# A long convolution and a state-space layer on one core: four more C blocks by DMA-transpose, and a new task order

## The chip, the cores and the metric

The kernel runs on one core of a Trainium2 chip. A core has TensorE (PE, matrix products into PSUM), VectorE (DVE), ScalarE (ACT), GpSimd (POOL) and SyncE (SP). Here POOL and SP do almost nothing but start DMA transfers, which sixteen DMA engines of the core carry out. The metric is device time in microseconds (us) of one execution, compared by medians.

## The reference

Two independent layers share one kernel. Each has 2048 positions and 1024 channels; the results stand side by side in an output of 2048 x 2048 in bf16.

```
# layer A: short convolution, gate, long convolution by FFT, gate
k_shift = sum over t<4 of k_pad[:, t:t+S, :] * shift_k[:, 3-t]
kv = k_shift * v
y = irfft(rfft(kv, 2S) * rfft(ssm_k, 2S))[:S] + kv * ssm_D
a = q * y
# layer B: complex diagonal state space
Lam_bar = exp(dt * Lam);  B_bar = ((Lam_bar - 1) / Lam)[:, None] * (B_re + i B_im)
Bu = einsum("bld,pd->blp", x, B_bar)
h_t = Lam_bar * h_(t-1) + Bu_t
b = 2 * einsum("blp,dp->bld", h, C_re + i C_im).real + x * Dskip
out = concatenate([a, b], axis=-1)
```

## The kernel before

Everything is cut into named tasks. A list of some 1,700 names, ORDER (lines 67 to 171), is written out by hand or by a planner beforehand; the kernel walks through it (`for task in ORDER.split()`) and issues each task's instructions. So every engine, and every engine's queue of transfers, gets its work in the order of this list, each waits only for its own next instruction, and the list decides which work stands in front of which. Nothing is planned at run time. Tasks carry indices after the name.

**Layer B** is done in sixteen chunks i of 128 positions. `bl.j.w` loads a block of B (j of eight, w real or imaginary), `bT` turns it by eight TensorE transposes into a PSUM tile of pool ps_t (two buffers), `bc` copies it to BT. The first ten such blocks are staged in the tile CT, which later holds C. `xl` and `xt` load and turn the first three chunks of x; `x.i` copies them to xT, or, from the fourth chunk, brings the chunk by DMA-transpose. `U.i.jp` (line 478) is 32 matmuls of 128 columns into ps_u (two buffers), `ue` (480) its copy on ScalarE. VectorE then does the recurrence of the chunk: `r1` (490, product with the table Z1), `r2` (499, sum), `ca` (504, carry), `sc` (510, two scans), `cm`, `cy` (carry for the next chunk), `r3` and `r4` (490, 523). `y.i.dh.part` (534, 539) is the product with C into ps_y (one buffer), each of the two halves dh in four parts; `ye` (549) copies it out and `yst` stores it, `ysh` for the last chunk. The tables come from `tab`, `sin`, `par_rest`, `z1`, `eo`, `stt`, `z2`, which use slots 5 to 7 of CT as working space until the last `stt` and `eo`.

**C** reaches CT in sixteen blocks (d of eight, w of two). A block goes one of two ways. Either `cl` (449) loads 256 KB into a staging buffer of tag ld (five buffers, shared with the last six B blocks and with `v`), `cT` (430) turns it with eight TensorE transposes and `cc` (453, ScalarE) copies it to CT; or `cx` (451) brings it by one DMA-transpose, issued from SP's queue, straight into CT:

```
E["cx"] = lambda d, w: nc.sync.dma_start_transpose(CT[:, :, w, d * P:(d + 1) * P], Cv[w][d * P:(d + 1) * P, :])
E["cT"] = lambda d, w: tr_(("cn", d, w), ("cp", d, w))
E["cc"] = lambda d, w: nc.scalar.copy(CT[:, :, w, d * P:(d + 1) * P], st.pop(("cp", d, w))[:])
```

A cx writes to all eight rows of CT, so it waits for the staged B blocks and for the tables. y.i.0 needs the blocks with d below 4, y.i.1 those from 4.

**Layer A** is an FFT in three stages over sixteen residues n2. `k` and `v` load; `kvm` (579), `kva` (586), `kvb` (592), `kvc` (597) on VectorE give kv in a tile acc (two buffers), `am.n2.w` (603) multiplies it with the table F1t into ps_a (three buffers), `ae` (612) copies, `ast` (POOL) stores to the DRAM tile Ys_kv. `hl`, `hT`, `hc`, `hm` (649), `he` (657), `hst` (664) do the same for the filter, with `hd` adding the skip term; tile ysbh has three buffers, Ys_h is the DRAM tile. Stage two, over 32 groups g: `lh`, `l`, `lw` load, `sh` and `sk` (684) multiply, `she` and `ske` copy to hab or hb and x16, `sw` (711, 712, POOL) swaps halves by DMA, `pr` (717, VectorE) multiplies, `sa` (726) goes back into ps_t, `sae` (737) copies into vsb (two buffers, two groups each), and `vst` (739, POOL) stores to the DRAM tile Vs. Every load `vl` of stage three needs all sixteen vst. Stage three: `vl`, `a3` (756), `a3e` (764), then `qm` (775) or, for the last three residues, `qp` (770) multiplies with q (`ql`), and `ost` or `oth` stores.

The remaining tasks `ld_*`, `wb`, `wbe`, `par_T`, `p32`, `exp`, `dve2`, `dve3`, `sm_pre`, `sin0`, `dd` are small and prepare parameters and weights.

Of the kernel before, what the change touches and what calls it, by code (L numbers as in the profile page):

```python
# [66 lines left out]
bl.0.1 bl.1.1 ld_w xl.0 k.-3 ld_par xl.1 ld_F bl.7.1 ld_G bl.0.0 k.-2 bT.0.1 bl.4.1 xl.2 bT.1.1 bc.0.1 k.-1 bl.2.1  # L67
wb.4 bc.1.1 bl.5.0 par_T wb.5 bl.4.0 p32 wb.6 bl.1.0 exp1 xt.0 bl.3.1 bl.2.0 xt.1 bl.3.0 wbe.4 dve2 k.0 x.0 bl.6.0
dve3 wb.7 x.1 x.3 wbe.5 bT.0.0 sm_pre exp2 wbe.6 hl.0.0 xt.2 wbe.7 bl.7.0 bc.0.0 tab.0 bl.5.1 wb.0 hl.0.1 wb.1 k.1 x.2
dd bT.7.1 wbe.0 bT.5.0 wbe.1 bl.6.1 tab.1 wb.2 wb.3 bc.5.0 v.0 bc.7.1 x.4 tab.2 bT.1.0 wbe.2 bT.2.1 wbe.3 bc.1.0 tab.3  # L70
k.2 x.5 bc.2.1 sin0 U.0.0 tab.4 hl.1.0 k.3 kvm.0 k.4 sin.2 bT.2.0 U.1.0 bc.2.0 ue.0.0 par_rest k.5 sin.4 bT.3.1 U.2.0
ue.1.0 kva.0 eo.0 bT.3.0 U.3.0 bc.3.1 bc.3.0 kvb.0 ue.2.0 stt.0 z1.1 bT.4.0 bT.4.1 kvm.1 ue.3.0 U.1.1 eo.1 U.3.1
ue.1.1 bc.4.1 k.6 bc.4.0 kva.1 z1.0 U.0.1 kvc.0 ue.3.1 kvb.1 eo.2 kvm.2 bT.6.0 bT.5.1 v.1 bc.6.0 am.0.0 U.2.1 ae.0.0
bc.5.1 ue.0.1 z1.2 kvm.3 bT.6.1 am.0.1 am.0.2 am.0.3 U.1.2 ae.0.2 ae.0.1 ue.2.1 stt.2 ast.0.0 ae.0.3 bT.7.0 ue.1.2
ast.0.1 bc.6.1 U.0.2 v.2 bc.7.0 stt.1 cl.0.1 cl.2.0 cl.1.0 U.0.3 kva.2 eo.3 kvc.1 ue.0.2 kvb.2 am.1.0 cl.2.1 ue.0.3
U.2.2 stt.3 kvc.2 z2 cT.2.0 r1.0 cl.3.1 cT.0.1 k.7 ae.1.0 U.3.2 cl.3.0 cc.2.0 cl.0.0 cx.5.0 ue.2.2 kva.3 cT.2.1 cc.0.1
U.2.3 cx.6.0 r2.0 ue.3.2 cc.2.1 hd.0 am.2.0 sc.0 k.8 hT.0.0 ue.2.3 cx.4.1 U.3.3 ae.2.0 hc.0.0 cx.7.1 am.2.1 am.1.1
ue.3.3 hT.0.1 ae.2.1 am.1.2 cx.7.0 cT.0.0 ae.1.1 ast.2.0 am.1.3 hc.0.1 U.1.3 ast.1.0 kvb.3 ae.1.2 cm.0 r3.0 ae.1.3
U.4.0 cc.0.0 ast.1.1 ue.1.3 kvm.4 cT.3.1 ue.4.0 cT.1.0 cc.3.1 hm.0.0.0 hm.0.0.1 v.3 hm.0.0.2 U.4.1 he.0.0.0 r4.0 k.9
he.0.0.1 cl.1.1 he.0.0.2 cx.6.1 hst.0.0.0 cy.0 kva.4 U.4.2 ue.4.1 cc.1.0 v.5 r1.1 cT.3.0 am.2.2 hm.0.0.3 cc.3.0 v.6  # L80
U.4.3 cx.4.0 kvc.3 ue.4.2 r2.1 he.0.0.3 ae.2.2 hT.0.2 v.4 hst.0.0.1 ue.4.3 U.5.0 ca.1 cx.5.1 sc.1 v.9 hm.0.1.0 am.2.3
ue.5.0 hm.0.1.1 U.5.1 hc.0.2 he.0.1.0 he.0.1.1 U.5.2 ae.2.3 hst.0.1.0 kvb.4 ue.5.1 cm.1 r3.1 ast.2.1 cT.1.1 ue.5.2
hT.0.3 cc.1.1 am.3.0 hm.0.1.2 hl.1.1 hm.0.1.3 x.6 U.5.3 kvm.5 ae.3.0 he.0.1.2 he.0.1.3 hl.2.0 hc.0.3 v.7 hst.0.1.1
hm.0.2.0 am.3.1 hm.0.2.1 r4.1 k.10 ue.5.3 y.0.0.0 he.0.2.0 he.0.2.1 y.0.0.1 kva.5 ae.3.1 hst.0.2.0 y.0.0.2 kvc.4 hd.1
am.3.2 kvm.6 y.0.0.3 ast.3.0 ae.3.2 am.3.3 am.4.0 ye.0.0 hm.0.2.2 hT.1.0 ae.3.3 y.0.1.0 ae.4.0 kvb.5 ast.3.1 he.0.2.2
kva.6 am.4.1 y.0.1.1 ae.4.1 r1.2 ast.4.0 hm.0.2.3 y.0.1.2 he.0.2.3 hc.1.0 hm.0.3.0 hst.0.2.1 y.0.1.3 he.0.3.0 kvc.5
hT.1.1 ye.0.1 cy.1 am.4.2 r2.2 v.8 hm.0.3.1 am.4.3 ae.4.2 yst.0 y.1.0.0 ae.4.3 kvb.6 he.0.3.1 am.5.0 ast.4.1 ca.2
y.1.0.1 kvc.6 ae.5.0 hst.0.3.0 kvm.7 v.11 hm.0.3.2 hm.0.3.3 k.11 am.5.1 he.0.3.2 U.6.0 x.7 he.0.3.3 ae.5.1 hst.0.3.1
hc.1.1 sc.2 v.13 am.5.2 y.1.0.2 k.12 ue.6.0 ast.5.0 ae.5.2 y.1.0.3 hm.1.0.0 am.5.3 ye.1.0 U.6.1 ae.5.3 he.1.0.0
ast.5.1 kva.7 hT.1.2 ue.6.1 hm.1.0.1 hm.1.0.2 am.6.0 r3.2 he.1.0.1 y.1.1.0 he.1.0.2 hst.1.0.0 ae.6.0 hm.1.0.3 U.6.2  # L90
# [749 lines left out]
```

## Time and profile before

| | |
|---|---|
| median of nine runs | 384.27 us (382.0 to 386.89) |
| the profiled execution, in all | 383.0 us |
| its span, first to last instruction | 380.9 us |
| TensorE busy | 362.2 us (95%) |
| VectorE busy | 329.9 us (87%) |
| ScalarE busy | 277.0 us (73%) |
| GpSimd busy | 124.9 us (33%) |
| moved by DMA | 101.15 MB, mean 266 GB/s |
| transposes on TensorE, line 430 | 112 from ld, 80 from CT, 24 from ysb |
| DMA-transposes | 13 for xT, 8 for CT |

The profile is of one execution. Its span is 2.1 us shorter than that execution's time. Busy shares are averages over stages that differ; matmuls are pipelined, and the end of one is modelled, so that the spacing between their starts says more than their lengths. A row of the windows gives, for a stretch of time, the busy microseconds of each engine, the granted TensorE clock, the share of time in which the sixteen DMA engines had packets, and what they moved. A wait row names who waited, for whom, how long in all, how often, and the longest.

### The profile page before, as it was taken

What the parts mean: (1) busy time and instruction counts of PE and PEld (TensorE: products, weight loads), DVE (VectorE), ACT (ScalarE), POOL (GpSimd) and SP (SyncE); (2) the same over time, 40 slices, a digit from 0 to 9 for tenths busy, and PEclk for the clock granted to TensorE, in tenths of its full rate; (3) what the DMA queues carried; (4) which work ended last, traced back from release to release, by engine and by line L of the source; (5) the groups of instructions that cost most, each with busy time, mean ns of one, the idle gap of its engine ahead of it and who ended that gap; (6) DMA issues with size and microseconds to landing.
All of it is one profiled execution on the core that took longest, in us unless ns stands there. A gap on an engine that the chain in (4) does not pass through costs nothing.

```text
span 380.9 us, 9007 instructions
## 1 busy us (share of the span) xinstructions
PE 362.2 (95%) x3553; PEld 247.5 (65%) x3553; DVE 329.9 (87%) x341; ACT 277.0 (73%) x511; POOL 124.9 (33%) x215
## 2 busy tenths in 40 slices
PE   4999999999999999999999999999999999799992
PEld 2699999966777767777666455545645755564440
DVE  3899989999999997999999999989983597099843
ACT  2889888778788777777427888998899988437232
POOL 3000102346365645547204322352342523102111
PEclk9999999999999999999999999999999999999998
DMA  8998699997686866455978989999999956889988
GB/s 245 336 322 246 179 214 258 258 338 245 213 269 244 214 168 199 148 189 172 315 178 264 266 300 278 359 285 296 313 282 360 303 200 189 295 299 361 405 326 293
DMA packets 60772, 101.15 MB, mean 266 GB/s; under 512 B 28445, under 2 KB 31517, under 8 KB 60730
## 3 DMA queue, kind: packets, MB, share of 16 engines
q1 hardware_dynamic: 47274, 59.51, 54.7%
q0 software_dynamic: 13376, 41.05, 31.0%
q8 instruction: 28, 0.46, 0.5%
q14 instruction: 14, 0.11, 0.1%
q10 hardware_dynamic: 80, 0.01, 0.0%
HBM read 53.10 MB, written 33.55 MB: 228 GB/s over the span
## 4 chain that ended last, share of the span: by engine, by line
PE 73%; DMA 9%; ACT 5%; DVE 5%; issue 4%; POOL 1%; SPq 0%; DVEq 0%; ACTq 0%; POOLq 0%
PE ps_u L478 24%; PE ps_y L534 23%; PE ps_a L684 5%; PE ps_t L726 5%; PE ps_t L430 3%; DMA Vs<-vsb 3%; PE ps_a L603 3%; DMA ysb<-in_B_x_dram 3%; PE ps_a L649 3%; PE ps_t L627 2%; PE ps_u L534 2%; DMA Ys_h<-ysbh 2%; PE ps_y L539 1%; PE ps_a L756 1%; DVE h L510 1%
## 5 line engine op out<-in xcount | busy, mean ns | idle before, releaser
L534 PE MATMUL ps_y<-CT,h 128*128 128x512 bf16 x480 | 125.1, 379 | 0.7 <-ACT yo L549 0.5
L478 PE MATMUL ps_u<-xT,BT 128*128 128x128 bf16 x2048 | 124.9, 220 | 0.0
L478 PEld LDWEIGHTS <-BT 128*128 128x128 bf16 x2048 | 120.1, 99 | 6.5 <-issue 0.2
L534 PEld LDWEIGHTS <-h 128*128 128x128 bf16 x512 | 46.3, 98 | 46.1 <-DVE h L523 0.7
L510 DVE TENSOR_TENSOR_SCAN h<-rtab,h 128x1024 bf16<-128x1024 f32 x32 | 71.5, 2277 | 0.3
L664 POOL DMA_DIRECT2D Ys_h<-ysbh x64 | 46.2, 724 | 39.2 <-ACT ysbh L657 39.0
L480 ACT CAST u<-ps_u 128x512 bf16<-128x512 f32 x64 | 38.5, 602 | 26.6 <-PE ps_u L478 26.6
L737 ACT CAST vsb<-ps_t 128x512 bf16<-128x512 f32 x64 | 39.1, 643 | 9.6 <-DMA Vs<-vsb 5.0
L490 DVE TENSOR_TENSOR mt<-u,Z 128x4096 bf16<-128x4096 bf16 x16 | 36.6, 2286 | 9.6 <-ACT u L480 9.6
L657 ACT CAST ysbh<-ps_a 128x512 bf16<-128x512 f32 x64 | 35.9, 611 | 10.3 <-DMA Ys_h<-ysbh 5.4
L614 POOL DMA_DIRECT2D Ys_kv<-ysb x32 | 17.9, 561 | 77.5 <-ACT ysb L612 75.4
L612 ACT CAST ysb<-ps_a 128x512 bf16<-128x512 f32 x64 | 37.1, 605 | 6.2 <-PE ps_a L603 5.8
L706 ACT CAST x<-ps_a 128x512 bf16<-128x512 f32 x64 | 37.7, 632 | 2.5 <-PE ps_a L684 2.4
L490 DVE TENSOR_TENSOR mt<-h,Z 128x4096 bf16<-128x4096 bf16 x16 | 36.6, 2285 | 0.1
L717 DVE TENSOR_TENSOR hab<-x,hab 128x2048 bf16<-128x2048 bf16 x18 | 21.7, 1215 | 10.4 <-DMA hab<-hab 6.7
L579 DVE TENSOR_TENSOR mt<-kring,wbc 128x4096 bf16<-128x4096 bf16 (+3 forms) x16 | 30.1, 1884 | 0.0
L549 ACT CAST yo<-ps_y 128x512 bf16<-128x512 f32 x30 | 18.2, 608 | 14.7 <-PE ps_y L534 12.8
L539 PE MATMUL ps_y<-Dd,xT 128*128 128x128 bf16 x120 | 26.3, 219 | 0.0
L726 PEld LDWEIGHTS <-wts 128*128 128x128 bf16 x128 | 12.3, 98 | 17.3 <-issue 4.4
L603 PE MATMUL ps_a<-acc,F1t 128*128 128x512 bf16 x64 | 22.1, 379 | 0.1
L694 ACT CAST hab<-ps_a 128x512 bf16<-128x512 f32 x36 | 21.3, 622 | 0.9 <-PE ps_a L684 0.7
L649 PE MATMUL ps_a<-hT,F1t 128*128 128x256 bf16 x128 | 21.3, 272 | 0.6 <-ACT ysbh L657 0.4
(125 smaller groups left out, 518.2 us busy)
## 6 DMA issues: line engine op xcount, KB each, us to landing
Ys_kv<-ysb POOLq DMA_DIRECT2D x32, 256.0 KB, 3.1
Ys_h<-ysbh POOLq DMA_DIRECT2D x64, 128.0 KB, 3.1
hk<-Ys_h SPq DMA_DIRECT2D x16, 512.0 KB, 6.2
l2k<-Ys_kv SPq DMA_DIRECT2D x16, 512.0 KB, 5.6
Vs<-vsb POOLq DMA_DIRECT2D x16, 512.0 KB, 6.0
vv<-Vs SPq DMA_DIRECT2D x32, 256.0 KB, 5.8
hab<-hab POOLq DMA_DIRECT2D x36, 128.0 KB, 5.6
kring<-in_A_k_dram SPq DMA_DIRECT2D x16, 256.0 KB, 5.3
```

What stands on the lines that cost most here:

```text
L478: nc.tensor.matmul(pu[:, w, jl, :], BT[:, 2 * jp + jl, w, d, :], xT[:, d, :], start=(d == 0), stop=(d == ND - 1))
L480: E["ue"] = lambda i, jp: nc.scalar.copy(st["u", i][:, :, 2 * jp:2 * jp + 2, :], st.pop(("pu", i, jp))[:])
L490: nc.vector.tensor_mul(m, s_, win(Z))
L510: nc.vector.tensor_tensor_scan(gf[:, a, :], rt1, gf[:, a, :], 0.0, ALU.mult, ALU.add)
L534: nc.tensor.matmul(py[:], h[:, 1 - w, j, :], CT[:, j, w, dh * 512:(dh + 1) * 512], start=(j == 0 and w == 0), stop=(j == NJ - 1 and w == 1))
L603: nc.tensor.matmul(st["pa", n2, w][:], F1t[:, cc, :], st["kv", n2][:, dh * 512:(dh + 1) * 512], start=True, stop=True)
L612: nc.scalar.copy(st["ysb", n2, cc][:, dh * 512:(dh + 1) * 512], st.pop(("pa", n2, w))[:])
L649: nc.tensor.matmul(pt[:, cc * DQ:(cc + 1) * DQ], F1t[:, cc, :], st["hT", qd, n4][:, w, :], start=True, stop=True)
L657: nc.scalar.copy(st["yh", qd, n4, w // 2][:, :, w % 2, :], st.pop(("pa", qd, n4, w))[:].rearrange("p (c d) -> p c d", c=2))
L664: gpd(Ys_h[cc, n0:n0 + 2, :, qd * DQ:(qd + 1) * DQ].rearrange("n k d -> k n d"), t_[:, cc, :, :])
L706: nc.scalar.copy(st["x16", g][:, w * 512:(w + 1) * 512], st.pop(("ps", "l2k", g, w))[:])
L737: nc.scalar.copy(st["vsb", gq][:, gi, w * 512:(w + 1) * 512], st.pop(("ps", "v", g, w))[:])
```

## The change

Only ORDER differs; all functions, buffers and sizes are the same. The tasks cl, cT and cc of the blocks with d = 2 and d = 3 are gone, and cx.2.0, cx.2.1, cx.3.0 and cx.3.1 are there instead: twelve blocks come by DMA-transpose and four (d = 0 and 1) by TensorE. In addition the whole list is in a new order, on every engine. Both lists are too long to show; these are the stretches around the first U, the C blocks, the residues 10 to 15 of layer A, the end of stage two, and the end.

```
-bl.0.1 bl.1.1 ld_w xl.0 k.-3 ld_par xl.1 ld_F bl.7.1 ld_G bl.0.0 k.-2 bT.0.1 bl.4.1 xl.2 bT.1.1 bc.0.1 k.-1 bl.2.1
-wb.4 bc.1.1 bl.5.0 par_T wb.5 bl.4.0 p32 wb.6 bl.1.0 exp1 xt.0 bl.3.1 bl.2.0 xt.1 bl.3.0 wbe.4 dve2 k.0 x.0 bl.6.0
-dve3 wb.7 x.1 x.3 wbe.5 bT.0.0 sm_pre exp2 wbe.6 hl.0.0 xt.2 wbe.7 bl.7.0 bc.0.0 tab.0 bl.5.1 wb.0 hl.0.1 wb.1 k.1 x.2
-dd bT.7.1 wbe.0 bT.5.0 wbe.1 bl.6.1 tab.1 wb.2 wb.3 bc.5.0 v.0 bc.7.1 x.4 tab.2 bT.1.0 wbe.2 bT.2.1 wbe.3 bc.1.0 tab.3
-k.2 x.5 bc.2.1 sin0 U.0.0 tab.4 hl.1.0 k.3 kvm.0 k.4 sin.2 bT.2.0 U.1.0 bc.2.0 ue.0.0 par_rest k.5 sin.4 bT.3.1 U.2.0
...
-U.2.2 stt.3 kvc.2 z2 cT.2.0 r1.0 cl.3.1 cT.0.1 k.7 ae.1.0 U.3.2 cl.3.0 cc.2.0 cl.0.0 cx.5.0 ue.2.2 kva.3 cT.2.1 cc.0.1
-U.2.3 cx.6.0 r2.0 ue.3.2 cc.2.1 hd.0 am.2.0 sc.0 k.8 hT.0.0 ue.2.3 cx.4.1 U.3.3 ae.2.0 hc.0.0 cx.7.1 am.2.1 am.1.1
...
-hT.3.2 hc.3.1 am.10.3 hm.3.0.0 hm.3.0.1 y.4.0.1 ae.10.3 kvb.12 he.3.0.0 r2.5 ast.10.1 am.11.0 he.3.0.1 hT.3.3 ae.11.0
...
-she.31.0 sa.27.0 cm.13 r3.13 ske.30.0 sa.27.1 she.31.1 U.14.2 ye.12.0 sw.31 sae.27.0 sae.27.1 cy.13 r4.13 sk.30.1
-sk.29.1 ue.14.2 vst.13 sa.28.0 ske.29.1 sk.31.0 sa.28.1 sae.28.0 pr.29 y.12.1.0 ske.30.1 sae.28.1 sk.31.1 pr.30
-ske.31.0 sa.29.0 ql.0 ske.31.1 sa.29.1 ql.5 ql.1 y.12.1.1 sae.29.0 ql.6 sae.29.1 ql.2 pr.31 ql.4 sa.30.0 vst.14
-sa.30.1 sae.30.0 y.12.1.2 sae.30.1 sa.31.0 sa.31.1 sae.31.0 U.15.1 sae.31.1 vst.15 y.12.1.3 ue.15.1 U.14.3 ye.12.1
...
-y.15.1.0 a3e.2.0 a3e.11.0 y.15.1.1 a3e.2.1 ye.15.0 qm.2 y.15.1.2 ql.14 ost.2 qp.15.0 ql.10 y.15.1.3 ql.11 qp.15.1
-ql.13 a3.14.0 qm.3 ye.15.1 a3.10.0 a3.14.1 ost.3 a3.11.1 a3.12.0 a3e.11.1 vl.13 a3e.10.0 ql.8 ql.12 oth.15.0 oth.15.1
-qm.11 ost.11 a3e.12.0 qp.14.0 qp.14.1 a3.8.0 oth.14.0 a3.10.1 oth.14.1 ysh.0 a3.12.1 ysh.1 a3e.10.1 a3e.12.1 a3.8.1
-qm.10 a3e.8.0 qm.12 ost.10 a3e.8.1 a3.13.0 ost.12 a3.13.1 qm.8 ost.8 qp.13.0 qp.13.1 oth.13.0 oth.13.1
...
+xl.0 xl.1 ld_w bl.0.1 bl.1.1 ld_par bl.3.0 ld_F bl.2.0 bl.1.0 ld_G k.-3 xt.0 bl.0.0 xl.2 xt.1 k.-2 x.0 k.-1 wb.0 x.1
+bl.5.0 wb.1 wbe.0 bl.3.1 par_T wb.2 wbe.1 x.3 p32 bT.1.1 exp1 bT.2.0 bc.1.1 k.0 wbe.2 bl.5.1 wb.4 dve2 bl.4.1 bc.2.0
+bT.1.0 dve3 bl.4.0 tab.0 k.1 wbe.4 bl.2.1 wb.5 bc.1.0 bl.6.0 xt.2 sm_pre bl.7.1 wbe.5 x.4 wb.6 exp2 bT.0.0 x.2 tab.1
+dd wb.7 hl.0.0 wbe.6 bT.0.1 bc.0.0 hl.0.1 k.2 k.3 wb.3 wbe.7 bc.0.1 bT.3.0 hl.1.0 sin0 bl.6.1 tab.2 U.0.0 x.5 tab.3
...
+bc.4.1 ue.0.1 stt.2 bT.6.1 ue.2.1 cT.0.0 U.1.2 kvm.2 z2 cc.0.0 cx.7.1 U.0.2 kvc.0 ue.1.2 kva.1 v.2 am.0.0 v.1 am.0.1
+ue.0.2 U.2.2 k.7 bc.6.1 ae.0.0 cx.4.0 ae.0.1 kvb.1 ast.0.0 kva.2 bT.7.0 cx.2.1 ue.2.2 U.3.2 bc.7.0 kvm.3 v.3 cx.2.0
+am.0.2 am.0.3 ue.3.2 U.0.3 ae.0.2 kvb.2 ae.0.3 cl.1.1 kva.3 ast.0.1 cx.5.1 U.3.3 ue.0.3 kvc.2 r1.0 cT.1.0 ue.3.3
+hT.0.0 cl.0.1 cc.1.0 U.1.3 cx.7.0 kvc.1 hc.0.0 r2.0 cx.3.1 am.1.0 am.1.1 ue.1.3 U.4.0 sc.0 ae.1.0 ae.1.1 v.5 ast.1.0
+k.8 am.1.2 cx.4.1 am.1.3 ue.4.0 U.4.1 ae.1.2 ae.1.3 cx.6.0 ast.1.1 am.2.0 hm.0.0.0 ue.4.1 cT.0.1 kvb.3 ae.2.0 cx.3.0
...
+hst.0.0.0 r4.0 am.2.2 k.9 hm.0.0.2 ue.2.3 cx.6.1 hT.0.2 ae.2.2 hm.0.0.3 hT.0.3 kvc.3 he.0.0.2 U.4.3 r1.1 he.0.0.3
+cx.5.0 hc.0.2 hst.0.0.1 hm.0.1.0 hl.1.1 hm.0.1.1 ue.4.3 v.4 hm.0.1.2 kva.4 U.5.0 v.8 v.6 cy.0 r2.1 U.5.1 ue.5.0 ca.1
...
+ye.4.0 am.10.0 hT.3.3 kva.12 he.2.3.2 y.4.1.0 he.2.3.3 ae.10.0 kva.13 hst.2.3.1 am.10.1 am.10.2 am.10.3 ae.10.1
+y.4.1.1 kvb.12 ae.10.2 ast.10.0 ae.10.3 kvc.11 hm.3.0.0 hm.3.0.1 x.10 y.4.1.2 he.3.0.0 ast.10.1 r1.5 he.3.0.1 am.11.0
+hm.3.0.2 hst.3.0.0 hm.3.0.3 x.12 ae.11.0 y.4.1.3 hc.3.2 kvc.12 am.11.1 U.9.0 he.3.0.2 r2.5 he.3.0.3 ae.11.1 hst.3.0.1
+ca.5 ye.4.1 am.12.0 sc.5 hm.3.1.0 ue.9.0 U.9.1 ae.12.0 ast.11.0 he.3.1.0 yst.4 am.11.2 hm.3.1.1 ue.9.1 am.11.3 U.9.2
+he.3.1.1 ae.11.2 hst.3.1.0 ae.11.3 kvb.13 am.12.1 hm.3.1.2 ue.9.2 cm.5 ast.11.1 hm.3.1.3 r3.5 U.9.3 he.3.1.2 he.3.1.3
+ae.12.1 hst.3.1.1 hc.3.3 am.12.2 hm.3.2.0 kvm.14 hm.3.2.1 ue.9.3 ast.12.0 ae.12.2 he.3.2.0 am.12.3 he.3.2.1 hm.3.2.2
+kvc.13 ae.12.3 hm.3.2.3 hst.3.2.0 r4.5 v.15 am.13.0 he.3.2.2 ast.12.1 kva.14 he.3.2.3 y.5.0.0 ae.13.0 hst.3.2.1
+am.13.1 kvm.15 y.5.0.1 ae.13.1 ast.13.0 am.13.2 am.13.3 hm.3.3.0 ae.13.2 y.5.0.2 ae.13.3 kvb.14 he.3.3.0 hm.3.3.1
+ast.13.1 kva.15 hm.3.3.2 y.5.0.3 he.3.3.1 hst.3.3.0 he.3.3.2 hm.3.3.3 kvc.14 he.3.3.3 r1.6 am.14.0 ye.5.0 am.14.1
+am.14.2 hst.3.3.1 ae.14.0 y.5.1.0 ae.14.1 am.14.3 ast.14.0 y.5.1.1 cy.5 kvb.15 ae.14.2 r2.6 ae.14.3 y.5.1.2 ast.14.1
+y.5.1.3 kvc.15 ca.6 am.15.0 sc.6 lh.0 am.15.1 am.15.2 ae.15.0 lh.2 U.10.0 ae.15.1 lh.1 ast.15.0 am.15.3 U.10.1 ue.10.0
...
+ske.29.0 r1.13 sk.29.1 sk.30.0 sae.28.0 sa.27.1 ske.29.1 sk.30.1 sa.28.1 sae.27.1 U.15.1 ske.30.0 vst.13 pr.29
+ske.30.1 sae.28.1 pr.30 sk.31.0 y.12.0.3 ske.31.0 ue.14.1 sk.31.1 r2.13 sa.29.0 ye.12.0 ql.6 sa.29.1 ql.0 ske.31.1
+ql.5 y.12.1.0 ca.13 sae.29.0 ql.1 pr.31 ql.2 sae.29.1 ql.4 sa.30.0 ue.15.1 vst.14 sa.30.1 sc.13 sae.30.0 y.12.1.1
+sae.30.1 sa.31.0 sa.31.1 sae.31.0 y.12.1.2 sae.31.1 U.15.2 vst.15 cm.13 r3.13 y.12.1.3 ue.15.2 U.15.3 ye.12.1 yst.12
...
+y.15.0.2 y.15.0.3 y.15.1.0 y.15.1.1 a3e.12.0 y.15.1.2 a3e.11.0 qm.8 y.15.1.3 a3e.11.1 a3e.10.0 ost.8 qm.11 a3e.10.1
+a3.13.0 ql.15 ost.11 ye.15.0 a3.15.0 qp.13.0 ye.15.1 a3.12.1 a3.13.1 qm.10 oth.13.0 a3e.12.1 ysh.0 a3.14.0 qp.13.1
+ost.10 a3.15.1 qm.12 a3.14.1 ost.12 qp.14.0 qp.14.1 oth.14.0 oth.13.1 qp.15.0 ysh.1 oth.14.1 qp.15.1 oth.15.0 oth.15.1
```

## The prediction

> **What bounds the kernel now.** I read the busy line and the slices first, then the chain of waits, then the windows, the wait list and the instructions in order of time. On the page, TensorE leads and the chain runs through it:
>
> ```profile
> PE 362.2 (95%) x3553; PEld 247.5 (65%) x3553; DVE 329.9 (87%) x341; ACT 277.0 (73%) x511; POOL 124.9 (33%) x215
> ...
> PE   4999999999999999999999999999999999799992
> ...
> PE 73%; DMA 9%; ACT 5%; DVE 5%; issue 4%; POOL 1%; SPq 0%; DVEq 0%; ACTq 0%; POOLq 0%
> ```
>
> Busy time of a pipelined PE is not proof, so I counted its work by spacing. The chain in order of time (start, length, engine, tile, line, count) gives unhindered runs:
>
> ```profile
> 38.96 0.65 PE ps_a L603 x3
> 39.60 1.79 PE ps_u L478 x32
> ...
> 47.41 0.89 PE ps_t L430 x16
> ...
> 81.59 0.86 PE ps_y L534 x4
> ```
>
> That is 56 ns for a 128-column matmul, 216 ns for a 512-column one. Over all groups of the page (2048 + 128 + 216 + 128 narrow ones, 512 + 64 + 128 + 128 + 64 wide ones, 128 of 256 columns, 8 of wb) the sum is 351 us. The span is 380.9. The other 30 us are: 3.3 before the first matmul; 11 until about 22 us (waits, and matmuls at half pace: eight transposes take 1.0 us there, 0.45 later, with the clock row at 1.00 throughout); 2.3 between 22 and 200 us; 6.7 after that; 7.0 after the last matmul. So TensorE has almost no hole to fill: a new order can lose much and win little. VectorE is full too, and transfers are full just where the C blocks come:
>
> ```profile
> 30.00:40.00 10.00, 10.00 (x172) 9.53 (x169) 9.90 (x11) 9.25 (x20) 0.00 (x0) 1.00 0.69 239
> 50.00:60.00 10.00, 10.00 (x166) 9.50 (x164) 8.47 (x9) 8.58 (x14) 1.62 (x3) 1.00 1.11 227
> 60.00:70.00 10.00, 10.00 (x171) 9.79 (x169) 9.93 (x9) 7.44 (x12) 2.92 (x4) 1.00 1.24 251
> 230.00:260.00 30.00, 30.00 (x219) 16.77 (x217) 28.21 (x23) 26.65 (x54) 11.71 (x22) 1.00 0.99 319
> ```
>
> (Window, length, then busy us of PE, PEld, DVE, ACT, POOL, clock, DMA share, GB/s.) Two stalls in the middle and at the end matter below:
>
> ```profile
> 152.19 0.69 DVE L592 TENSOR_TENSOR acc<-mt 128x1024 bf16<-128x1024 bf16 x1 [2.49 <-PE ps_a L603]
> ```
>
> ```profile
> ACT ysbh L657 <- DMA Ys_h<-ysbh: 5.4, 5, 2.2
> ...
> ACT vsb L737 <- DMA Vs<-vsb: 5.0, 3, 3.6
> ...
> PE ps_t L726 <- ACT vsb L737: 3.2, 2, 2.6
> ```
>
> **The change, part by part**, against the profiled execution (span 380.9, 383.0 in all, 1.3 under the median 384.27).
>
> 1. *TensorE transposes removed.* Four cT tasks, 32 transposes: 4 x 0.45 = **-1.8 us** of the 351. PE is packed there, so I take all of it; bounds -1.8 and 0 (if PE then waits for something else).
>
> 2. *Copies removed.* Four cc on ScalarE at 1.03 us (L453): -4.1 us on an engine busy 7.4 to 9.3 of 10 us. No PE wait of before names them: 0; bounds -1 and 0.
>
> 3. *Transfers.* Four loads of 256 KB (cl) go, four DMA-transposes (cx) come. On SP's queue a cl takes 0.4 us, a cx 1.24 to 3.5 (eight took 14.9 in all), so about +6 us of a queue that paused for about 2 us three times between 31 and 44 us and for over 3 at 71 to 75. Between 50 and 70 us the DMA share is 1.11 and 1.24 at 227 and 251 GB/s; at 319 GB/s the share was 0.99. By bytes those windows would have needed 0.70 and 0.78: 8.7 us too much over eight transposes, 1.1 us each, +4.4 us for four more. The cover is the slack at 30 to 50 (share 0.69, 0.67) and the late use: the first y task reads C at 78.4 us. In the new order the last cx that y.0.0.0 needs (cx.3.0) follows cT.1.0's buffer (about 51 us) behind four others: 51 + 5 x 2.4 (48.76 to 53.5 held two) + 6.1 to land = 69, and PE reaches y.0.0.0 at about 75. Behind them wait k.9, hl.1.1, v.4; kvc.4 wants v.4 near 81. Cost 0; bounds 0 and +5 (the 8.7 repeated, less that slack).
>
> The row says 0.45 us of TensorE and 1.03 of ScalarE per block against 4.2 to 6.1 us of landing by DMA. [...]
>
> The order moves nearly every task on POOL's queue too, but its issues are the same in both (Ys_h, Ys_kv, Vs, hab, outputs); I price them only where a buffer turns on them (5 and 6).
>
> 4. *Start.* U.0.0 began at 19.31. New order: xt first, six bT instead of seven before U.0.0. Walking the two ps_t buffers by the rows (1.0 us for eight cold transposes, 1.01 ACT and 0.69 DVE per evacuation): wb.0 at 7.0 as before (its weights land then), bT.1.1 at 8.8, bT.1.0 at 11.2, xt.2 at 12.4 to 13.7 (its load has 2.9 MB ahead instead of 2.6), then bT.0.0, bT.0.1, bT.3.0: U.0.0 at 17.0 to 18.2. PE's own work ahead of it is 0.45 less, already counted, so **-0.9**; bounds -1.9 and +1.5 (a load one landing row, 1.5 us, later).
>
> 5. *The middle.* PE and VectorE take turns: kvb.n needs the acc buffer that am.(n-2).3 frees, am.n needs kvc.n. Before, am.10.3 ended and kvb.12 started at once (the 152.19 row), and y.5.0.0 needed r4.5: VectorE had 18.3 us of work on that way, PE 18.4. It cost nothing. In the new order, from am.10.3 to am.15.0 PE has 16 hm + 16 am + 4 U + 11 y parts = 3.5 + 3.5 + 7.2 + 10.0 = 24.2 us; VectorE from kvb.12 to kvc.15 has 4 kvb, 5 kvc (0.60), 2 r1 and r3 (2.20), 2 r2 and r4 (1.14), 2 kvm (2.27), 2 kva (1.13), a scan pair (4.40) and 0.3 = 26.9. So PE must wait **+2.7** between 150 and 185 us; queued behind am.13 to am.15 stand U.10 and y.6, and ScalarE's copies, the last stores of Ys_kv and so the loads of stage two wait for them. Before lost 2.2 there (1.5 at 130 to 145 behind the Ys_h wait, 0.7 after). Whether the Ys_h wait returns is open: bounds +0.5 and +2.5; I take **+0.7**, as the ring of ysbh has longer turns there now (10.9 and 9.1 us for 8.8 and 12.4, but 4.2 again at one).
>
> 6. *The convolution's second stage.* A vsb buffer turns through ACT, POOL and a store of Vs; PE stalls on the third sa after it. Shortest turns in PE work: before 8.1 (it took 10.7: the stall of 2.6), 7.7 (took 8.4), 10.4; now 7.4, 8.9, 8.9, 9.6, 9.8. At a turn of 9.6 that is 2.2 + 0.7 + 0.7 = 3.6, against 3.4 before; Behind a waiting sa stand y.12 and U.15 parts, and the last Vs store, for which all vl loads wait, comes later by as much. I take **+0.5**; bounds -2.4 (turn 8.4) and +5.5 (10.7 everywhere).
>
> 7. *The end.* After y.15.1.3 there are seven a3 halves now, eleven before (work counted in 1's total); before, two of the last waited 0.9 and 0.6 for ACT and DVE, and the last qt came by DMA. Now ql.15 waits for qm.11. **-0.5**; bounds -1.5 and +1.0.
>
> Sum: -1.8 + 0 + 0 - 0.9 + 0.7 + 0.5 - 0.5 = **-2.0 us**: span 378.9, 381.0 for the profiled execution, 382.3 on the median. 0.5% is 1.9 us, about what this kernel's measurement can tell from no change (nine runs span 382.0 to 386.9).
>
> **The rivals.**
>
> A. *Slower: the vsb turn.* If each short turn takes the 10.7 us of before's last one, stalls are 3.3 + 1.8 + 1.8 + 1.1 + 0.9 = 8.9 instead of 3.4: -2.5 + 5.5 = +3.0, **387.3**. For it: landings of Vs stores reach 8.9 us, and six windows there have a DMA share of 0.98 or more. Against: the 10.7 held 2.7 us of POOL waiting to issue. It decides for slower from a turn of about 10.5 us.
>
> B. *No change: VectorE keeps the time.* The removed 1.8 us lie on an engine that must wait for kvc.15 anyway; with the Ys_h wait back (part 5 at +2.5) the sum is -0.2, **384.1**. For it: VectorE is at 10.00 in nearly every window from 70 to 150. Against: it has its own holes at 280 to 330.
>
> C. *Slower: the transposes come late.* If the eight's landing is doubled by the queue, cx.3.0 lands near 79 instead of 69 and y.0.0.0 waits 4: -2.0 + 4 = +2, **386.3**; k and v loads behind would add to it. Against: PE had no hole of 0.1 us between 50 and 80 us with DMA share 1.24.
>
> D. *The better end:* start -1.9, middle +0.5, vsb -1, tail -1.5: -5.7, near **378.6**.
>
> **How the numbers follow.** Forecast (380.5 to 382.4) 0.30; D 0.15; B 0.23; A 0.20; C and like delays 0.12. So faster 0.45, same 0.23, slower 0.32. The point is 382.3. The range takes in D, B, most of A and C: 378.6 to 388.5; the likeliest case alone has 380.5 to 383.5.
>
> **What would show it.** L430 of ld x80 instead of x112 and L453 x4; a first U matmul at 17 to 18.2 us; y.0.0.0 near 75 with no DMA wait on CT; a PE wait for VectorE (acc or h) of 2 to 3 us between 150 and 185; L726 waits for vsb of 3 to 4 us in all; under 7 us after the last matmul. Wrong if PE has holes of several us at 40 to 80, a first U after 19.5 us, or L726 waits above 6.

## The result and the profile after

The changed kernel is slower: median 388.01 us (18 executions, 384.95 to 392.57) against 384.61 us of the kernel before (55 executions), ratio 1.0078 with a 95% interval of 1.0056 to 1.0099, so about +3.0 us, +3.4 by the medians. Ratios, and the means of groups of executions below, leave out executions that took over 1.5% more than the fastest of their kernel; two of these 18 did. The point of the prediction, 382.3, stood on the other side of no change; the time lies inside its range.

The profiled execution after took 389.62 us, 1.6 above its median, while that of before was 1.6 below its own (384.61; 1.3 below the 384.27 of the nine executions known before). So the two traces differ by 7.0 us of span (380.9 and 387.9), twice the difference of the medians. What makes such an execution long is itself a finding below.

The page of the changed kernel, its busy line, its slices of TensorE and of the granted clock, and the chain by engine:

```profile
PE 365.0 (94%) x3521; PEld 245.7 (63%) x3521; DVE 330.1 (85%) x341; ACT 273.7 (71%) x507; POOL 125.0 (32%) x215
...
PE   4999999999999999989999999999999999999692
...
PEclk9999999999999999989999999999999999999988
...
PE 59%; DMA 16%; DVE 9%; issue 7%; ACT 4%; POOL 2%; SPq 1%; DVEq 0%; ACTq 0%; POOLq 0%
```

TensorE has 32 matmuls less and is yet busy 2.8 us longer; its slices show a dip near 175 us and a hole near 365, and the clock row dips near 170 us and right behind the hole, where the row of before has 9 up to its last slice.

To see where the time went I took the spacing of TensorE's starts, less 56, 108 or 216 ns by its width for each matmul, and summed what is left over by stretch:

| us | work | to 30 us | 30 to 110 | 110 to 190 | 190 to 340 | 340 to last matmul | after it | span |
|---|---|---|---|---|---|---|---|---|
| before | 350.3 | 14.4 | 0.3 | 2.1 | 4.5 | 2.1 | 7.2 | 380.9 |
| after | 348.5 | 13.4 | 0.3 | 6.9 | 4.3 | 7.4 | 7.1 | 387.9 |
| predicted difference | -1.8 | -0.9 | 0 | +0.7 | +0.5 | -0.5 (with the tail) | | -2.0 |
| difference | -1.8 | -1.0 | 0 | +4.8 | -0.2 | +5.2 | | +7.0 |

The first four parts of the sum came as predicted, and the stretch of the vsb turns (190 to 340 us) within 0.7; the middle and the end did not. Windows of the changed kernel (window, length, busy us of PE, PEld, DVE, ACT, POOL, clock, DMA share, GB/s):

```profile
50.00:60.00 10.00, 10.00 (x165) 9.39 (x163) 9.96 (x8) 8.02 (x13) 1.08 (x2) 1.00 1.23 230
...
170.00:180.00 10.00, 9.59 (x43) 4.39 (x43) 10.00 (x11) 7.07 (x14) 7.20 (x12) 0.83 0.49 166
...
360.00:370.00 10.00, 6.81 (x31) 2.85 (x29) 8.61 (x8) 2.25 (x4) 2.72 (x5) 0.93 0.95 321
```

The DMA share is high where the DMA-transposes run, as foreseen, and TensorE has no hole there. Then the end, VectorE in order of time (start, length, engine, line, operation, count):

```profile
362.81 2.29 DVE L490 TENSOR_TENSOR mt<-h,Z 128x4096 bf16<-128x4096 bf16 x1
365.02 2.49 DVE L775 TENSOR_TENSOR ot<-ot,qt 128x1024 bf16<-128x1024 bf16 x4
367.43 1.22 DVE L523 TENSOR_TENSOR h<-mt 128x2048 bf16<-128x2048 bf16 x1
```

and TensorE beside it:

```profile
364.91 0.59 PE L756 MATMUL ps_t<-vv,Gt 128*128 128x512 bf16 x2
368.70 0.61 PE L534 MATMUL ps_y<-CT,h 128*128 128x512 bf16 x1 [3.19 <-DVE h L523]
369.10 0.31 PE L539 MATMUL ps_y<-Dd,xT 128*128 128x128 bf16 x1
369.21 1.06 PE L534 MATMUL ps_y<-CT,h 128*128 128x512 bf16 x2
```

r3.15 ends; then VectorE does four qm (L775), because the new list has them ahead of r4.15 (L523); only then comes h, for which y.15.0.0 stands waiting. From its last start TensorE pauses 3.36 us beyond the pace. And the matmuls behind the pause run at half pace until 372.0: 0.85 us for two wide ones instead of 0.43, 1.6 us in all. In the kernel before, one qm (qm.6) stood between r3.15 and r4.15:

```profile
358.20 0.68 DVE L775 TENSOR_TENSOR ot<-ot,qt 128x1024 bf16<-128x1024 bf16 x1
358.80 1.22 DVE L523 TENSOR_TENSOR h<-mt 128x2048 bf16<-128x2048 bf16 x1
```

There TensorE had y.14.1 to do until 360.10 us, and y.15.0.0 followed without a pause.

Waits of the changed kernel (waiter, releaser: total, number, longest):

```profile
ACT ysbh L657 <- DMA Ys_h<-ysbh: 7.0, 7, 1.4
...
PE ps_y L534 <- DVE h L523: 4.1, 2, 3.2
...
ACT vsb L737 <- DMA Vs<-vsb: 3.1, 2, 2.0
...
DVE acc L592 <- PE ps_a L603: 2.9, 3, 1.6
...
PE ps_t L726 <- ACT vsb L737: 0.7, 1, 0.7
```

The waits of TensorE for h are new. The vsb wait, from which rival A was made, has fallen from 3.2 to 0.7 us. VectorE's waits for acc, 4.0 us in two pieces before (the longer one 2.49), are 2.9 us in three now, so they have not grown.

### The profile page after: what moved, and what is told of

Read it like the earlier page. It is cut to its first block, busy times and chain, and to the rows that moved or that the text cites. A ratio compares the mean times of both kernels' runs of the same rounds, so it can differ in the third digit from the quotient of the medians.

```text
span 387.9 us, 8931 instructions
## 1 busy us (share of the span) xinstructions
PE 365.0 (94%) x3521; PEld 245.7 (63%) x3521; DVE 330.1 (85%) x341; ACT 273.7 (71%) x507; POOL 125.0 (32%) x215
## 4 chain that ended last, share of the span: by engine, by line
PE 59%; DMA 16%; DVE 9%; issue 7%; ACT 4%; POOL 2%; SPq 1%; DVEq 0%; ACTq 0%; POOLq 0%
PE ps_u L478 22%; PE ps_y L534 17%; DMA Vs<-vsb 5%; PE ps_a L684 4%; PE ps_t L726 3%; PE ps_a L603 3%; PE ps_t L430 3%; PE ps_a L649 2%; DVE h L510 2%; DMA hab<-hab 2%; DMA Ys_h<-ysbh 2%; DVE mt L490 2%; PE ps_t L627 2%; DMA qt<-in_A_q_dram 2%; DMA ysb<-in_B_x_dram 2%
## 5 line engine op out<-in xcount | busy, mean ns | idle before, releaser
L534 PE MATMUL ps_y<-CT,h 128*128 128x512 bf16 x480 | 127.6, 386 | 4.5 <-DVE h L523 4.1
L737 ACT CAST vsb<-ps_t 128x512 bf16<-128x512 f32 x64 | 37.2, 625 | 8.1 <-PE ps_t L726 3.5
L717 DVE TENSOR_TENSOR hb<-x,hb 128x2048 bf16<-128x2048 bf16 x14 | 17.0, 1218 | 12.4 <-ACT x L706 7.8
```

What stands on the lines that cost most here:

```text
L534: nc.tensor.matmul(py[:], h[:, 1 - w, j, :], CT[:, j, w, dh * 512:(dh + 1) * 512], start=(j == 0 and w == 0), stop=(j == NJ - 1 and w == 1))
L717: nc.vector.tensor_mul(hab[:], st.pop(("x16", g))[:].unsqueeze(1).to_broadcast([P, 2, D]), hab[:])
L737: nc.scalar.copy(st["vsb", gq][:, gi, w * 512:(w + 1) * 512], st.pop(("ps", "v", g, w))[:])
```

## The experiments

The first theory (W): the loss comes from the new order, mostly from where tasks stand on VectorE's queue, and the DMA-transposes are a gain. The rival (T): the four more DMA-transposes cost transfers that are not covered. All times are medians, ratios against the kernel before on the same chip.

**One task moved: e1_r4_early.**

```
-r3.15 a3e.2.0 a3.2.1
+r3.15 r4.15 a3e.2.0 a3.2.1
...
-qm.7 qm.9 ost.7 qm.3 ost.9 qm.2 ost.3 r4.15 ql.8
+qm.7 qm.9 ost.7 qm.3 ost.9 qm.2 ost.3 ql.8
```

> The new order with one task moved: r4.15 stands right behind r3.15 on VectorE, ahead of qm.7, qm.9, qm.3 and qm.2. Theory W (the loss is made by VectorE's place in the new list): the wait of y.15.0.0 for h (3.2 us in the profile after) and the slow matmuls behind it (about 1.2 us) go, some 0.5 us come back where the four qm finish later, so about 384 us, 383 to 385.5. Rival T (the four more DMA-transposes cost the time): nothing changes, 388. Rival N (TensorE would be slow at that place anyway): 386.8, the wait goes and the slow matmuls stay.

Measured 383.6 us, ratio 0.9982 (0.9952 to 1.0012): 4.4 us less than the changed kernel by the medians, 3.7 by the ratios, as W said. VectorE and TensorE there:

```profile
362.08 1.23 DVE L523 TENSOR_TENSOR h<-mt 128x2048 bf16<-128x2048 bf16 x1
363.23 2.49 DVE L775 TENSOR_TENSOR ot<-ot,qt 128x1024 bf16<-128x1024 bf16 x4
```

```profile
363.37 0.39 PE L534 MATMUL ps_y<-CT,h 128*128 128x512 bf16 x1 [0.91 <-DVE h L523]
...
363.65 0.59 PE L534 MATMUL ps_y<-CT,h 128*128 128x512 bf16 x2
```

The pause is 1.07 us instead of 3.36, nearly the 2.4 us of the four qm, and y.15 runs at full pace behind it. Moving one task past four thus takes away the whole measured loss: with it the new order isn't slower than the old.

**The transposes alone in the old order: e2_c_alone.**

```
-stt.3 kvc.2 z2 cT.2.0 r1.0 cl.3.1 cT.0.1 k.7 ae.1.0 U.3.2 cl.3.0 cc.2.0 cl.0.0 cx.5.0 ue.2.2 kva.3 cT.2.1 cc.0.1
+stt.3 kvc.2 z2 cx.2.0 r1.0 cT.0.1 k.7 ae.1.0 U.3.2 cl.0.0 cx.5.0 ue.2.2 kva.3 cx.2.1 cc.0.1
...
-kvm.4 cT.3.1 ue.4.0
+kvm.4 cx.3.1 ue.4.0
...
-r1.1 cT.3.0 am.2.2
+r1.1 cx.3.0 am.2.2
```

> The order of before, with the blocks d = 2 and 3 by DMA-transpose at the places where cT stood (cl and cc of them left out). Theory W: 32 transposes less on TensorE and nothing else, 384.6 - 1.8 = 382.8 us, 382 to 383.5. Rival T: the transposes cost 4.4 us of transfers that are not covered, 384.6 - 1.8 + 4.4 = 387.2 us, and y.0.0.0 waits for CT.

Measured 384.3 us, ratio 0.9982 (0.9947 to 1.0017), so -0.7 us with -2.0 to +0.7: T's +2.6 is out, and the -1.8 lies just inside. By the sums of spacing TensorE's work fell by the 1.8, and 0.9 came back at 30 to 110 us.

**All sixteen blocks by DMA-transpose: e5_all_dma.**

```
-ue.2.1 cT.0.0 U.1.2 kvm.2 z2 cc.0.0 cx.7.1
+ue.2.1 U.1.2 kvm.2 z2 cx.0.0 cx.7.1
...
-r1.0 cT.1.0 ue.3.3 hT.0.0 cl.0.1 cc.1.0 U.1.3
+r1.0 cx.1.0 ue.3.3 hT.0.0 U.1.3
...
-ue.4.1 cT.0.1 kvb.3
+ue.4.1 cx.0.1 kvb.3
...
-cT.1.1 ue.4.2 hT.0.1 cc.1.1 kvm.4
+cx.1.1 ue.4.2 hT.0.1 kvm.4
```

> The new order with the last four blocks (d = 0 and 1) by DMA-transpose as well, so all sixteen. Theory W: 388.0 - 1.8 = 386.2 us, and less if TensorE then only waits for VectorE in the middle (387.5). Rival T: another 4.4 us of transfers less 1.8, 390.6 us, with a wait of y.0.0.0 for CT.

Measured 388.6 us, ratio 1.0097 (1.0059 to 1.0135): not different from the changed kernel. Neither T's loss nor W's whole gain: TensorE's 1.8 us went, and 1.1 came back at 30 to 110 us, the most of it as a pause for VectorE:

```profile
78.70 1.22 PE L626 MATMUL ps_t<-ident,hk 128*128 128x128 bf16 x16 [0.77 <-DVE hk L641]
```

**The order alone: o1_order_alone and o2_order_r4.** The second has the edit of e1_r4_early in addition; the loads that were moved for the ld buffers are named in the expectation.

```
-bT.7.0 cx.2.1 ue.2.2
+bT.7.0 cl.2.1 ue.2.2
...
-kvc.2 r1.0 cT.1.0 ue.3.3
+kvc.2 cl.1.1 r1.0 cT.2.1 cc.2.1 ue.3.3
...
-ae.2.0 cx.3.0 U.4.2
+ae.2.0 cT.3.1 cc.3.1 U.4.2
```

> The new order with the blocks d = 2 and 3 by TensorE again (cl in the place of cx, cT and cc some tasks later; cT.1.0, cl.1.1, cl.0.1, v.3 and v.7 moved a little, so that the five ld buffers turn). Theory W: the order is the whole loss, and the four DMA-transposes give little in it, since VectorE holds the middle: 388.0 to 389.8 us. Rival T (the four DMA-transposes cost time): 388.0 + 1.8 - 4.4 = 385.4 us.

> o1_order_alone with r4.15 right behind r3.15, so the new order without the wait at the end and without the four more DMA-transposes; against e1_r4_early (383.6) it shows what the four are worth in the new order. By the 32 transposes alone: 383.6 + 1.8 = 385.4 us. If the distance of 2.8 between o1_order_alone and the changed kernel is theirs: 386.4 us. If VectorE holds the middle and hides them: 383.6 us.

Measured 390.83 us, ratio 1.0147 (1.0105 to 1.019), and with r4.15 early 388.47 us, ratio 1.0091 (1.0056 to 1.0126). Rival T has fallen: without the four DMA-transposes the new order is slower still. By the ratios they are worth 4.2 us there (1.0091 against 0.9982, some 1.8 us either way), more than the 1.8 of their TensorE work. VectorE in o2_order_r4 shows one way of this: the transposes stand ahead of am tasks, and VectorE waits for the acc buffers.

```profile
47.14 0.69 DVE L592 TENSOR_TENSOR acc<-mt 128x1024 bf16<-128x1024 bf16 x1 [1.16 <-PE ps_a L603]
...
75.02 0.69 DVE L592 TENSOR_TENSOR acc<-mt 128x1024 bf16<-128x1024 bf16 x1 [0.60 <-PE ps_a L603]
```

In e1_r4_early the first of these is 0.72 and the second isn't there. Since some loads had to be moved too, the 4.2 isn't the price of the transposes alone.

**Wait or slow matmuls: e8_half and e9_fill.** Two tests of the half pace behind the pause.

In e8_half:

```
-qm.7 qm.9 ost.7 qm.3 ost.9 qm.2 ost.3 r4.15
+qm.7 qm.9 r4.15 ost.7 qm.3 ost.9 qm.2 ost.3
```

and in e9_fill:

```
-r4.15 ql.8 ost.2 ql.13 ql.10 ql.12 y.15.0.0
+r4.15 ql.8 ost.2 ql.13 ql.10 ql.12 fill.15 y.15.0.0
...
+    def fill(n):
+        pt = ptile("ps_a", [P, 512])
+        for _ in range(n):
+            nc.tensor.matmul(pt[:], F1t[:, 0, :], CT[:, 0, 0, 0:512], start=True, stop=True)
+    E["fill"] = fill
```

> The new order with r4.15 behind qm.7 and qm.9, ahead of qm.3 and qm.2 only. The four qm ran without a pause for 2.4 us before r4.15, so the wait of y.15.0.0 should fall from 3.36 to about 2.2 us. Theory W with slow matmuls only after a long wait (those after 2.6 to 2.9 us in other runs were followed by none, those after 3.35 by ten slow ones): the wait loses 1.2 and the slow matmuls 1.6 us, 388.0 - 2.8 = 385.2 us. If matmuls are slow after any wait of 2 us: 386.8. If the loss at the end has nothing to do with the queue of VectorE: 388.

> The new order with 15 matmuls of 512 columns put ahead of y.15.0.0, whose product nobody reads: 15 x 0.216 = 3.24 us of work in the time in which TensorE waits for h. If the slow matmuls of y.15 come from the pause of TensorE, they go, while h comes as late as before: 388.0 - 1.6 = 386.4 us with more work. If they have another reason: 388.0 us, y.15 still slow.

Measured 385.28 us (ratio 0.9987, 0.9951 to 1.0024) and 385.81 us (ratio 1.0029, 1.0 to 1.0057). In e8_half the pause is 2.15 us and the matmuls behind it run at full pace (two wide ones in 0.43 us). In e9_fill TensorE does 15 matmuls more than the changed kernel and the whole is 1.9 us shorter by the ratios; h comes 2.4 us behind r3.15 as in the changed kernel, but nothing is slow behind it:

```profile
364.54 3.40 PE L764 MATMUL ps_a<-CT,F1t 128*128 128x512 bf16 x15
367.90 0.39 PE L534 MATMUL ps_y<-CT,h 128*128 128x512 bf16 x1
...
368.19 0.59 PE L534 MATMUL ps_y<-CT,h 128*128 128x512 bf16 x2
```

So here the pause makes the slow matmuls, and the end's loss has two terms: the wait and its echo.

**The middle: e6_am_up and e10_mid.**

In e6_am_up, beside the edit of e1_r4_early and the shorter moves of am.0.2, am.0.3 and am.7.3:

```
-kvm.12 hc.3.0 y.4.0.1 he.2.2.2 y.4.0.2 he.2.2.3 kvm.13 hm.2.3.2 hst.2.2.1 hm.2.3.3 y.4.0.3
+kvm.12 hc.3.0 am.10.0 y.4.0.1 ae.10.0 he.2.2.2 am.10.1 y.4.0.2 ae.10.1 he.2.2.3 kvm.13 am.10.2 hm.2.3.2 hst.2.2.1
+hm.2.3.3 am.10.3 y.4.0.3 ae.10.2
...
-ye.4.0 am.10.0 hT.3.3 kva.12 he.2.3.2 y.4.1.0 he.2.3.3 ae.10.0 kva.13 hst.2.3.1 am.10.1 am.10.2 am.10.3 ae.10.1
+ye.4.0 hT.3.3 kva.12 ast.10.0 he.2.3.2 y.4.1.0 he.2.3.3 kva.13 hst.2.3.1
```

and on top of that in e10_mid:

```
-ye.4.1 am.12.0 sc.5 hm.3.1.0 ue.9.0 U.9.1 ae.12.0 ast.11.0 he.3.1.0 yst.4 am.11.2 hm.3.1.1 ue.9.1 am.11.3 U.9.2
+ye.4.1 am.11.2 am.12.0 sc.5 ue.9.0 ae.11.2 am.11.3 ae.12.0 U.9.1 ae.11.3 hm.3.1.0 yst.4 kvb.13 ue.9.1 he.3.1.0
...
-ue.9.3 ast.12.0 ae.12.2
+ae.12.2 ue.9.3 ast.12.0
```

> e1_r4_early, and in addition six am tasks (am.0.2, am.0.3, am.7.3, am.10.0 to am.10.3) moved up on TensorE by one U or by some 1.5 to 3 us of its work, with their copies ae: kvb.2, kvb.9 and kvb.12 waited for the acc buffers that these free, 0.7, 0.8 and 2.4 us in the profile of e1_r4_early. Theory W (VectorE is the bound from 46 to 189 us, and what it waits for there is lost): 383.6 - 2.5 = 381.1 us, 380 to 382.5. Rival P (TensorE's own stalls, behind the Ys_h stores and the ps_a buffers, keep the time there): 383.6 us, no change.

> e6_am_up, and in addition am.11.2 and am.11.3 moved up past U.9.1 with their copies, and ae.12.2 put ahead of ue.9.3 on ScalarE: in the profile of e6_am_up VectorE waits 1.5 us for am.11.3 at kvb.13 in place of the 2.4 us at kvb.12, and TensorE 1.1 us at am.12.3 for ae.12.2. Theory W: those two go, the middle then loses about 1 us more than the start's offset, 383.3 - 1.5 = 381.8 us. Rival P (each wait that goes comes back at the next turn of the acc buffers): 383.3 us, no change against e6_am_up.

Measured 383.78 us, ratio 0.9955 (0.9921 to 0.9989), and 384.01 us, ratio 0.9981 (0.9945 to 1.0016). The first ends faster than the kernel before, but can't be told from e1_r4_early; the second brings nothing on top. Both times lie near P's numbers (383.6 and 383.3), not at W's (381.1 and 381.8). In e6_am_up VectorE's wait came back one turn later:

```profile
162.03 0.69 DVE L592 TENSOR_TENSOR acc<-mt 128x1024 bf16<-128x1024 bf16 x1 [1.49 <-PE ps_a L603]
```

and in e10_mid VectorE has none over 0.25 us between 50 and 190 us; the time didn't follow. TensorE's own loss at 110 to 190 us went from 6.6 (e1_r4_early) to 5.0 (e6_am_up). So VectorE's waits for acc may account for one or two of the 4.5 us by which e1_r4_early still loses more there than before, but the times don't show it; what the 4.5 hang on isn't settled. Its largest pieces are pauses of 0.8 and 0.6 us behind ysbh near 112 and 118 us, and one of 1.11 us at am.12.3 behind ScalarE.

**Parts of both orders: h_z2 and h_start.** The edits are too long to show: the first 45 or 30 us of the new list, then what is left in the order of e2_c_alone.

> The new order up to z2 (about 45 us), then all that is left in the order of before with the twelve DMA-transposes of e2_c_alone. Theory W: the gain of the start (1.0 us in the offsets of the two profiles) and that of the transposes, without middle and end of the new order: 384.6 - 1.0 - 1.8 = 381.8 us, 380.8 to 383.5. Rival T: 387.2 - 1.0 = 386.2 us.

> The new order as far as bc.7.1 (about 30 us; cl.0.0 left for later), then all that is left in the order of before with the twelve DMA-transposes of e2_c_alone. The border lies earlier than in h_z2, where v.0 and the last B blocks came late and TensorE lost 6.6 us at 40 to 50 us. Theory W: the start gains its 1.0 to 2 us (the first U of the new order began at 16.8 to 18.7 us in six profiles, that of the old at 19.3 and 19.9), nothing of the new order's middle and end is in it: about 382.5 us, faster than both kernels. If the gain of the start is only a shorter wait that VectorE takes back: 383.9 us, as e2_c_alone by its ratio. If the border costs again: above 385 us.

Measured 388.99 us, ratio 1.0122 (1.0086 to 1.0158), and 385.92 us, ratio 1.0024 (0.9986 to 1.0062). Both miss W's numbers, and neither says what a start is worth: the seam costs more. h_z2 loses 9.0 us at 30 to 110 us where VectorE comes late; behind the pauses of 1.67 and 2.26 us the matmuls are slow until 51 us (clock 0.71 in the window of 40 to 50 us), and nothing of it is won back in the 330 us behind:

```profile
41.63 0.81 PE L603 MATMUL ps_a<-acc,F1t 128*128 128x512 bf16 x3 [1.50 <-DVE acc L597]
42.68 0.38 PE L603 MATMUL ps_a<-acc,F1t 128*128 128x512 bf16 x1 [0.24 <-ACT ysb L612]
45.16 1.01 PE L430 MATMUL ps_t<-ident,ld 128*128 128x128 bf16 x8 [2.10 <-DVE BT L442]
```

The profile of h_start showed something else, at the end of stage two, which is in the old order:

```profile
330.94 1.87 PE L726 MATMUL ps_t<-hb,wts 128*128 128x512 bf16 x4 [3.04 <-ACT vsb L737]
332.60 2.49 PE L478 MATMUL ps_u<-xT,BT 128*128 128x128 bf16 x32
```

After a pause of 3.20 us, four wide matmuls take 1.66 us to the next start and 32 narrow ones 2.55 instead of 1.79. In the profile of e2_c_alone the same place paused 2.59 us and all was at full pace:

```profile
325.13 1.08 PE L726 MATMUL ps_t<-hb,wts 128*128 128x512 bf16 x4 [2.43 <-ACT vsb L737]
326.05 1.95 PE L478 MATMUL ps_u<-xT,BT 128*128 128x128 bf16 x32
```

**The wait at the edge: e13_vsb.**

```
-sa.30.0 vst.14 sa.30.1 sae.30.0 y.12.1.2 sae.30.1 sa.31.0 sa.31.1 sae.31.0 U.15.1 sae.31.1 vst.15 y.12.1.3 ue.15.1
+sa.30.0 vst.14 sa.30.1 sae.30.0 y.12.1.2 sae.30.1 U.15.1 y.12.1.3 sa.31.0 sa.31.1 sae.31.0 sae.31.1 vst.15 ue.15.1
```

> e2_c_alone with U.15.1 and y.12.1.3 put ahead of sa.31.0 on TensorE: 2.66 us of work in the place where sa.31 waits 2.59 us for the vsb buffer. Theory V (that wait stands at the edge of what makes the following matmuls slow, and this is why the executions of the old order have two mean clocks, 0.988 to 0.991 and 0.993 to 0.995, some 2.7 us apart): the wait goes, about 1 us comes back where a3.4.0 then waits for vl.4, and all executions have 0.993 or more, median 381 to 382.5 us, faster than both kernels. Rival S (what is moved only makes TensorE wait longer for the loads vl, and the two clocks have another reason): 384 us, and still two groups.

Measured 384.03 us, ratio 0.9958 (0.9921 to 0.9995), so faster than the kernel before, by 1.6 us, and than the changed one; from e2_c_alone (0.9982) the ratio can't tell it. Of V the clock came nearly true: eleven of twelve executions had a mean granted clock of 0.993 or more, one had 0.985 (387.88 us). Of e2_c_alone's executions, five had 0.988 to 0.991 (mean 384.9 us) and five 0.993 or more (382.7). The kernel before falls apart in the same way: over the five sets of comparisons, 51 executions at 0.991 or less with a mean of 385.6 us, 53 at 0.992 or more with 384.0. V's time didn't come, and S's 384 did: the stretch after 340 us lost 3.6 us instead of 2.1, 1.1 of it a pause at an a3 task, so part of what was won at sa.31 was lost to the loads behind.

## Why the prediction was wrong

The step that failed first is part 7, "The end", priced at -0.5 with bounds of -1.5 and +1.0. It counted the a3 halves that follow y.15 and the waits after the last matmul, and didn't walk VectorE's queue ahead of r4.15. The four qm were in the list to be read; at 0.60 us each they are 2.4 us, and e1_r4_early shortened the pause by 2.3. The stretch lost 5.2 us more than before: some 2.3 for those, 1.6 of slow matmuls, and some 1.3 of other waits of y.13 to y.15, which e1_r4_early has too (it loses 1.9 more there than before). Without this one item the new order has a ratio of 0.9982, about -0.7 us against the -2.0 predicted.

Part 5, the middle, failed too: +0.7 with bounds of +0.5 and +2.5, measured +4.8 in the profiled execution and +4.5 in e1_r4_early. Its mechanism was a wait of TensorE for VectorE of 2 to 3 us between 150 and 185 us. No such wait is there: the waits that the profile names for TensorE's matmuls in this stretch are 1.3 us, all for ScalarE (the longest 0.94 us at am.12.3); beside them a weight load waits 0.7 us for h. What the runs show in its place: the Ys_h wait did return (the question that the text left open), 7.0 us in all on ScalarE against 5.4; TensorE lost 5.2 us between 150 and 180 us, against 0.4 before; and 1.7 of these 5.2 are matmuls at half pace up to 174.0 us, a term that the sum didn't have at all, and one of chance, since e1_r4_early has the same tasks there at full pace (its mean clock is 0.996, the changed kernel's 0.988). The balance counted work only, as if each engine ran on without a pause whenever the other was ahead. What the rest of the middle's loss hangs on stays open.

Part 1 held (350.3 to 348.5 us of work), but "I take all of it" was too simple for the time: the same 1.8 us was worth 0.7 in the old order, nothing for the last four blocks, and more than itself in the new order with its tighter turns. Part 2 held. Part 3 held: no transfer came late.

```profile
73.29 1.61 PE L478 MATMUL ps_u<-xT,BT 128*128 128x128 bf16 x26
74.74 0.38 PE L534 MATMUL ps_y<-CT,h 128*128 128x512 bf16 x1
```

y.0.0.0 (74.74, "near 75") follows U without a gap. So rival C had no ground. Nor did four blocks more on TensorE pay: o2_order_r4, which has them, is slower than e1_r4_early (ratio 1.0091 against 0.9982). Part 4 held: the first U began at 18.3 us, -1.0 against -0.9. Part 6 is near in its sum (-0.2 against +0.5, inside its bounds) and wrong in its way, so by luck: the vsb waits fell to 0.7 us of the 3 to 4 foreseen, and TensorE lost the rest at other places. Rival A, the forecast of a slower kernel, came near the time by a mechanism that didn't occur. Rival B's engine was the right one, VectorE, but at the wrong place.

## What to carry to other kernels

When a list sets the order, walk each in-order queue from the last producer back to the task that the critical engine waits for, and price everything that stands between; four tasks of 0.6 us outweighed all the rest of a new order. Look at the tail above all, where little work is left to hide a wait. And a pause can have an echo, here 1.3 to 1.7 us of matmuls at half pace behind it: more work in the gap can be cheaper than the gap, as in e9_fill, where 15 matmuls more left the whole 1.9 us shorter.

## What the hardware showed that was not expected

A pause of TensorE can cost more than its length. The pauses of over 2.5 us in these profiles and what followed: 2.59, 2.75 and 2.90 us, full pace; 3.20, 3.35 and 3.36, half pace for 2.8 to 3.5 us, 1.3 to 1.7 us lost; another of 3.35 (o1_order_alone), full pace. Two stretches of half pace came behind several shorter pauses close together (the changed kernel at 170 us, h_z2 at 45 us). In e5_all_dma the slow stretch began only 1.2 us after the pause had ended. The windows' clock falls with it: 0.83 in the slice of 170 us, 0.93 in that of 360.

The granted clock in the traces sorts these pauses. It changes in steps: in the traces of both kernels every change lies a whole number of times 3.413 us after the first record (in the kernel before 104 times from 22.24 to 377.23 us; in the changed kernel 44 times from 20.37 to 170.56 us, 57 times from 173.97 to 368.53). Ahead of the first record the windows have 1.00, which the prediction read, while the matmuls there ran at half pace (eight transposes in 1.0 us against 0.45). Windows laid on these steps, first the changed kernel, then o1_order_alone with as long a pause:

```profile
365.12:368.53 3.41, 0.39 (x2) 0.00 (x0) 3.41 (x5) 0.15 (x1) 2.18 (x4) 1.00 0.95 276
368.53:371.94 3.41, 3.24 (x10) 1.37 (x11) 0.79 (x2) 0.00 (x0) 0.00 (x0) 0.50 0.98 324
```

```profile
366.59:370.01 3.42, 1.42 (x9) 0.77 (x10) 1.94 (x3) 0.00 (x0) 1.51 (x3) 1.00 0.98 260
370.01:373.42 3.41, 3.41 (x19) 1.64 (x18) 1.27 (x2) 1.07 (x2) 0.54 (x1) 1.00 1.02 388
```

The work of TensorE in such a step, each matmul counted at 56, 108 or 216 ns and split where a step begins inside it, beside the clock of the next one:

| trace, start of the step | work in its 3.41 us | clock in the next |
|---|---|---|
| changed kernel, 365.12 | 0.23 | 0.50 |
| h_start, 326.90 | 0.84 | 0.50 |
| h_z2, 40.70 | 0.86 | 0.50 |
| changed kernel, 167.14 | 1.26 | 0.50 |
| e5_all_dma, 366.05 | 1.29 | 0.50 |
| o1_order_alone, 366.59 | 1.40 | 1.00 |
| kernel before, 322.61 | 1.41 | 1.00 |
| e8_half, 365.04 | 1.51 | 1.00 |

The five of these steps with 1.29 us or less are followed by half the clock, the three with 1.40 or more by the full one. Of the 207 steps at full clock up to the last matmul in the traces of the two kernels, the two of the changed kernel in the table alone are followed by 0.50; the other 205 hold 1.41 us or more. How far this goes beyond these traces isn't shown. The two pauses of 3.35 us, in e5_all_dma and o1_order_alone, have the same length and lie in steps with 1.29 and 1.40 us of work; and e1_r4_early has the same tasks at 167 us as the changed kernel, at full pace.

These steps fit the spread between executions of one kernel too: a step at half clock takes 0.0045 off the mean clock of 381 us and, as an estimate, up to 1.7 us of time (half of 3.41), and the two groups of executions of the kernel before are 0.0046 and 1.7 us apart. By the author's estimate they come from the wait of some 3 us at the end of stage two, which leaves its step now a little less work and now a little more: in the profiled execution that step held 1.41 us; e13_vsb, without that wait, has one execution of twelve in the lower group; in the kernel before itself the wait alone wasn't taken away.
